# Six places instead of four for the split parameters of a state-space kernel

## The chip, the core and the metric

The kernel runs on one core of a Trainium2 chip. The metric is the device time of one execution in microseconds (us). The kernel before took 372.38 us (median of three runs, 372.26 to 373.49). The engines are named as in the profile: PE (matrix products; PEld is its weight load), ACT (ScalarE), DVE (VectorE), POOL (GpSimd) and SP (SyncE, which only issues transfers here). Each engine works through its own instructions in their order; semaphores hold an instruction back until another engine or a transfer (DMA) has done its part.

## The reference, cut to what matters

Two branches are mixed with a gate per position: 2,048 positions, 640 channels, bfloat16.

```python
g = sigmoid((x * gate_w).sum(-1, keepdims=True))
# a: attention over 8 positions, 2 apart; 32 heads of 20 channels
qkv = x @ wqkv;  a = softmax(q . k[pos - 2*w]) weighted v  @ wo
# b: state-space convolution, N = 192 states a channel
logdA = exp(log_dt) * (A_re + 1j * A_im)
K = Re(einsum(C, exp(logdA * l), exp(log_dt) * B))      # l = 0 .. 2047
b = irfft(rfft(x padded) * rfft(K padded)) + x * Dskip
return g * a + (1 - g) * b
```

(The middle lines are shortened to their meaning.) The parameters A, B and C are 640 x 192 each, and the change concerns what is made of them before K can be computed.

## The kernel before

**Parameters.** `SSMParams.build` (L573 on) brings the complex parameters into a form of phase and size for every channel and state: `tau`, `x1` (phase), `xa`, `xl` (size) and `at` (angle), each a float32 tile of 128 x 960 (five blocks of 128 channels by 192 states). PE will need them in bfloat16, so each is split into two or three bfloat16 pieces whose sum is the value. `piece` (L650 to 659) makes one of the twelve pieces in three steps:

- ACT rounds the current value to a bfloat16 tile `pc` (L655, a copy of 128 x 960),
- SP stores this tile in the DRAM tensor `Sprm` (L657, 240 KB),
- where another piece follows, DVE subtracts `pc` from the value (L659); what is left goes into a scratch tile `s` and is the next piece's value.

The `pc` tiles come from the pool `sp_pc` (L582). A place is free again when its transfer to `Sprm` has landed and the subtraction has read it; the next copy that is given this place waits for both. Which place that is, is settled when the program is built, by the order in which places are given back in the program; it isn't a strict rotation. With the order of this kernel, the twelve copies wait for transfers as follows (counted in ACT's order):

| copy | 1 to 4 | 5 | 6 | 7 | 8 | 9 | 10 | 11 | 12 |
|---|---|---|---|---|---|---|---|---|---|
| waits for the transfer of piece | none | 1 | 4 | 2 | 5 | 6 | 7 | 3 | 8 |

**What stands beside it.** In the same stretch PE turns the input `x` with products with the identity (`ar` <- `ident`,`xn`, L252; evicted by ACT or DVE into `bufA`), computes the gate's sums (L268), and projects q, k and v: groups of five matmuls of 128 x 512 into a PSUM tile `tb` (L339, in `plan_late`, L317 on). There are two `tb` places; each group is evicted by ACT (L512) or DVE (L514) into `pv` or `prj`, and POOL's queue stores what belongs together (L354) into `qS`, `kS` and `vS` in DRAM and loads windows from there (`qc` and `kc` L381, `vc` L389). DVE's first products q times k are `prod` (L395). When all twelve pieces have landed, SP loads the matrices `L` from `Sprm` (L765), PE multiplies them with constants (L792), and ACT turns these into sines and exponentials (L804, L806) from which K is summed. The Fourier transforms and the mix with the gate follow in `fft_conv` (L1009 on).

**What sets the order.** A planner (`Plan`, L68 on) holds every step as a task with an engine, an expected duration, a due time, dependencies and the places that it takes and gives back, and plays them through (`order`, L98). Its list `SLOTS` (L75) has its own number of places for each pool, `"pc": 4` among them. `emit` (L198) then writes the instructions in the played order and ties every engine to it, so no engine leaves the order at run time.

Of the kernel before, what the change touches and what calls it, by code (L numbers as in the profile page):

```python
# [572 lines left out]
class SSMParams:  # L573
# [5 lines left out]
    def build(self, ctx, tc, pl, A_re, A_im, B_re, B_im, C_re, C_im, log_dt, gate_w, ident, gw_sb, pa, xl, wl):  # L579
        nc = tc.nc  # L580
        pin = ctx.enter_context(tc.tile_pool(name="sp_in", bufs=1, side="right"))
        pcs = ctx.enter_context(tc.tile_pool(name="sp_pc", bufs=4, side="right"))  # L582
        SH = [128, 5, NST]
        t = {}

# [765 lines left out]
```

## Time and profile before

One execution was profiled. Its views give times from the span's start.

| | |
|---|---|
| profiled execution | 372.98 us, span of its instructions 371.2 us |
| median of the runs | 372.38 us |
| busy share of the span: PE, DVE, ACT, POOL | 82%, 86%, 82%, 27% |
| mean granted clock of PE | 0.93 of full speed |
| transfers `Sprm` <- `pc` | 12, issued from 24.2 to 64.1 us, 3.5 to 8.4 us from issue to landing, median 7.3 |
| the copies `pc`, L655 | 12, about 1.00 us each, from 23.2 to 63.1 us |
| DMA share in the stages 30 to 40, 40 to 50, 50 to 60 us | 0.89, 1.06, 0.83 |

A timeline lists an engine's instructions by start; in brackets stands how long the engine was idle before one and what ended the wait. A table of waits sums these. The windows view gives the busy time of each engine within chosen stretches, the granted clock there (1.00 is full speed) and how busy the 16 DMA engines were; its share can pass 1 in this count. Busy time of PE is modelled at its ends, so that a gap in its timeline tells more than its share.

### The profile page before, as it was taken

To read this page: it belongs to the slowest core of one execution; us is meant where nothing else is said; L and a number is where in the kernel's file an instruction comes from. 1 tells how busy PE (TensorE), PEld (TensorE's weight loads), DVE (VectorE), ACT (ScalarE), POOL (GpSimd) and SP (SyncE) were. 2 spreads that over 40 slices of the span, in tenths; PEclk is the share of its full clock that TensorE was granted. 3 is DMA by queue.
4 is the path that set the end of the run, shared out by engine and by line. 5 is a ranking of instruction groups with operands and counts; after the bars stand their busy time and mean duration, and the time that the engine had idled before them with its cause. 6 is when DMAs were issued, how large, how long until landed. Compare 5 with 4: busy or idle time off the path is not lost. (4 is left out here: it accounts for less than half of the span.)

```text
span 371.2 us, 12265 instructions
## 1 busy us (share of the span) xinstructions
PE 303.6 (82%) x5286; PEld 176.0 (47%) x5286; DVE 319.6 (86%) x431; ACT 305.4 (82%) x417; POOL 98.4 (27%) x134
## 2 busy tenths in 40 slices
PE   0189499999999998896888888988989899988770
PEld 0155265444454444443344444546656656557660
DVE  2897969866999999999798999999889759999972
ACT  1499877468899899999799989979878698998881
POOL 8932332302003012236157001010110014310032
PEclk9999789999999998997595699989999999999985
DMA  8957988765346362759567833443464039943037
GB/s 259 369 153 190 255 214 245 226 193 171 106 96 183 116 131 85 166 124 216 90 199 158 195 92 86 104 92 106 124 225 145 13 113 221 252 93 72 4 91 197
DMA packets 53130, 57.26 MB, mean 154 GB/s; under 512 B 32596, under 2 KB 44692, under 8 KB 52820
## 3 DMA queue, kind: packets, MB, share of 16 engines
q0 software_dynamic: 8784, 31.20, 31.4%
q1 hardware_dynamic: 42260, 24.43, 26.0%
q10 hardware_dynamic: 2032, 0.85, 0.9%
q8 instruction: 41, 0.67, 0.8%
q14 instruction: 13, 0.11, 0.1%
HBM read 36.69 MB, written 19.77 MB: 152 GB/s over the span
## 5 line engine op out<-in xcount | busy, mean ns | idle before, releaser
L339 PE MATMUL tb<-bufA 128*128 128x512 bf16 x300 | 75.0, 391 | 6.2 <-ACT pv L512 4.8
L792 PE MATMUL ar<-Rarg,L 64*128 64x304 bf16 (+1 forms) x480 | 58.1, 299 | 15.4 <-ACT big L806 7.1
L804 ACT ACTIVATE big<-ar 128x608 bf16<-128x608 int16 x96 | 59.8, 679 | 10.1 <-PE ar L792 9.1
L395 DVE TENSOR_TENSOR prod<-qc,kc 128x2048 bf16<-128x2048 bf16 x40 | 47.3, 1218 | 5.7 <-PE lg L401 3.3
L339 PEld LDWEIGHTS <-bufA 128*128 128x128 bf16 x300 | 33.1, 121 | 37.1 <-issue 15.4
L806 ACT ACTIVATE big<-ar 128x864 bf16<-128x864 f32 x60 | 49.1, 900 | 1.4 <-PE ar L792 1.1
L462 DVE TENSOR_TENSOR pv<-vc,asb 128x2048 bf16<-128x2048 bf16 x40 | 47.3, 1217 | 1.5 <-PE tb L468 1.3
L792 PEld LDWEIGHTS <-L 64*128 64x128 bf16 x480 | 22.2, 97 | 50.4 <-issue 46.5
L1053 PEld LDWEIGHTS <-PHI 128*128 128x128 bf16 x288 | 26.2, 97 | 17.1 <-issue 8.7
L486 PE MATMUL tb<-wo_sb,oT 128*128 128x320 bf16 x160 | 28.7, 314 | 0.2
L845 PE MATMUL kps<-qq,pt 128*32 128x22 bf16 (+1 forms) x2560 | 26.4, 176 | 2.5 <-issue 1.1
L389 POOL DMA_DIRECT2D vc<-vS x16 | 11.7, 749 | 62.6 <-DVE pv L462 57.3
L845 PEld LDWEIGHTS <-pt 128*32 128x32 bf16 (+1 forms) x2560 | 22.7, 93 | 10.7 <-issue 7.3
L512 ACT ACTIVATE prj<-tb 128x512 bf16<-128x512 f32 x30 | 17.7, 597 | 7.8 <-PE tb L339 7.8
L468 PE MATMUL tb<-pv,ind 128*64 128x512 bf16 (+1 forms) x192 | 22.7, 358 | 1.6 <-DVE pv L462 1.3
L829 DVE TENSOR_TENSOR qq<-big 128x1408 bf16<-128x1408 bf16 x24 | 21.2, 882 | 0.0
L512 ACT ACTIVATE sp_k<-fp 128x1280 bf16<-128x1280 f32 x14 | 17.3, 1237 | 3.9 <-PE fp L1053 3.4
L252 PE MATMUL ar<-ident,xn 128*128 128x128 bf16 x80 | 8.3, 273 | 14.4 <-DMA xn<-in_A_x_dram 13.9
L1053 PE MATMUL fp<-bufA,PHI 128*128 128x320 bf16 x112 | 17.5, 298 | 3.2 <-ACT sp_k L512 2.2
L486 PEld LDWEIGHTS <-oT 128*128 128x128 bf16 x160 | 13.9, 101 | 8.4 <-issue 2.2
L401 PE MATMUL lg<-prod,ind 128*32 128x512 bf16 x160 | 16.6, 426 | 1.4 <-DVE prod L395 1.4
L827 DVE TENSOR_TENSOR pt<-big 128x1024 bf16<-128x1024 bf16 x24 | 16.4, 685 | 1.3 <-PE kps L845 0.7
(174 smaller groups left out, 599.7 us busy)
## 6 DMA issues: line engine op xcount, KB each, us to landing
vc<-vS POOLq DMA_DIRECT2D x16, 327.5 KB, 5.8
PHI<-c_phi POOLq DMA_DIRECT2D x8, 384.0 KB, 5.7
Sprm<-pc SPq DMA_DIRECT2D x12, 240.0 KB, 7.3
L<-Sprm SPq DMA_DIRECT2D x80, 36.0 KB, 3.6
kc<-kS POOLq DMA_DIRECT2D x8, 337.5 KB, 4.9
xn<-in_A_x_dram SPq DMA_DIRECT2D x4, 640.0 KB, 9.1
qc<-qS POOLq DMA_DIRECT2D x8, 320.0 KB, 5.6
Usb<-in_A_x_dram POOLq DMA_DIRECT2D x8, 320.0 KB, 5.2
```

Of the source, the lines that this page charges most:

```text
L339: nc.tensor.matmul(ppf, self.wq[:, kt, which * D + e:(which + 1) * D:5], self.xT[:, c0 // 1024, kt, c0 % 1024:c0 % 1024 + SC], start=(kt = ...
L395: nc.vector.tensor_tensor(b[e][:], b["qc"][:, e, :].unsqueeze(1).to_broadcast([128, W, C]), win(b["kc"][:, e, :], 0, W, DIL, C), ALU.mult)
L462: nc.vector.tensor_tensor(b["pv", e][:, :, :, k, :], for_e, aw, ALU.mult)
L468: nc.tensor.matmul(b["op", e][64 * a:64 * a + 64, 0:n, :], self.twin, b["pv", e][:, a, w, 0:n, :], start=(w == 0), stop=(w == HV - 1), ski ...
L486: nc.tensor.matmul(apf[:, :320], b["oT"][:, e, i * 128:(i + 1) * 128], wo_sb[:, e, hf * 320:(hf + 1) * 320], start=(e == 0), stop=(e == 4))
L512: nc.scalar.activation(o, i, ACT.Identity)
L792: nc.tensor.matmul(ar[:, g2, a0:a0 + ncol], L[rows, sb, gp, l0:l0 + 128], R[rows, c0:c0 + ncol], start=True, stop=True, tile_position=(64 ...
L804: nc.scalar.activation(dst[:, 2 * gp:2 * gp + 2, sub, :], ar[:].bitcast(I16)[:, :, 0:2 * SW:2], ACT.Sin, scale=SCL)
L806: nc.scalar.activation(dst[:, 2 * gp:2 * gp + 2].rearrange("p g s n -> p g (s n)"), ar[:, :, 0:2 * EW], ACT.Exp)
L829: nc.vector.tensor_tensor(qq[:], trg[:, :, KI:].rearrange("p a (v m) -> p a v m", v=2), exq[:, :, KI:].unsqueeze(2).to_broadcast([128, 32, ...
L845: nc.tensor.matmul(kps[32 * g:32 * g + 32, h, NM * ql:NM * ql + NM], pt[rows, k, v, :], qq[rows, k, v, :], start=(g not in started), stop= ...
L1053: nc.tensor.matmul(o.rearrange("p (c x) -> p c x", x=32), phis[fb][:, fl, kind, :], B[:, :, 2 * f1 + ri].rearrange("p c q g -> p c (q g)") ...
```

## The change

The pool of the `pc` tiles gets six places instead of four:

```diff
-        pcs = ctx.enter_context(tc.tile_pool(name="sp_pc", bufs=4, side="right"))
+        pcs = ctx.enter_context(tc.tile_pool(name="sp_pc", bufs=6, side="right"))
```

The planner's own `"pc": 4` stays, so the order that it plays stays too: in the built programs all five engines have the same instructions in the same order. Each place is 1,920 bytes in each partition, so the pool takes 3,840 bytes more. The addresses of ten of the twelve `pc` tiles differ; nothing else moved. In the built program the copies now wait for transfers so:

| copy | 1 to 6 | 7 | 8 | 9 | 10 | 11 | 12 |
|---|---|---|---|---|---|---|---|
| waits for the transfer of piece | none | 1 | 4 | 2 | 5 | 6 | 7 |

## The prediction, made before the changed kernel ran

> **What bounds the kernel now.** I read the page's slices first: from 37 to 55 us PE has a dip (4 tenths) and the granted clock two low slices (7 and 8 tenths), while DVE and ACT stay busy. So I asked for the waits of the stretch 18 to 80 us, and from there the timelines of ACT, PE and DVE. The waits (engine and line, what it waited for, us in total, times, longest):
>
> ```profile
> PE tb L339 <- ACT pv L512: 4.8, 3, 4.4
> ...
> ACT pc L655 <- DMA Sprm<-pc: 1.0, 1, 1.0
> ```
>
> PE's longest stop, 4.4 us, waits for an eviction by ACT. Of the twelve piece copies (L655) exactly one waits for a transfer, for 1.0 us. ACT's timeline (start, length, operation, in brackets the idle time before it and its releaser) shows that the one stands ahead of the other:
>
> ```profile
> 36.28 1.00 ACT L655 ACTIVATE pc<-s 128x960 bf16<-128x960 f32 x1
> 37.19 0.58 ACT L512 ACTIVATE pv<-tb 128x512 bf16<-128x512 f32 x1
> 37.79 1.28 ACT L635 ACT_TABLE_LOAD   x1
> 39.08 1.00 ACT L635 ACTIVATE at<-t 128x960 f32<-128x960 f32 x1
> 41.05 1.00 ACT L655 ACTIVATE pc<-s 128x960 bf16<-128x960 f32 x1 [0.96 <-DMA Sprm<-pc]
> 41.96 0.99 ACT L655 ACTIVATE pc<-x 128x960 bf16<-128x960 f32 x1
> 42.85 1.06 ACT L512 ACTIVATE pv<-tb 128x512 bf16<-128x512 f32 x2
> ```
>
> The sixth copy starts at 41.05 after 0.96 us of waiting; the seventh and two evictions of `tb` stand behind it on ACT. PE's timeline:
>
> ```profile
> 37.82 1.24 PE L339 MATMUL tb<-bufA 128*128 128x512 bf16 x5 [0.24 <-ACT pv L512]
> 43.48 4.43 PE L339 MATMUL tb<-bufA 128*128 128x512 bf16 x10 [4.42 <-ACT pv L512]
> 47.70 1.06 PE L252 MATMUL ar<-ident,xn 128*128 128x128 bf16 x8
> 48.55 1.66 PE L339 MATMUL tb<-bufA 128*128 128x512 bf16 x5
> 50.05 0.61 PE L252 MATMUL ar<-ident,xn 128*128 128x128 bf16 x8
> 50.50 2.32 PE L339 MATMUL tb<-bufA 128*128 128x512 bf16 x10
> ```
>
> Both `tb` places are full from 39.06 on; PE goes on at 43.48, right after the first of the two evictions, and from there it shows no gap until 82.15. In the stages 54 to 78 us it is busy 24.00 of 24 us at clock 1.00. So PE bounds this stretch, and its start at 43.48 hangs on ACT, which hangs on the transfer. Ten matmuls took 4.43 us here; 25 took 5.63 at 54.66, about half the time each. The windows show why (start:end, length, busy PE, PEld, DVE, ACT, POOL, then granted clock, DMA share, GB/s):
>
> ```profile
> 39.15:42.56 3.41, 0.00 (x0) 0.00 (x0) 3.27 (x5) 2.45 (x3) 2.48 (x4) 1.00 1.09 237
> 42.56:45.97 3.41, 2.49 (x6) 0.85 (x6) 3.31 (x4) 3.35 (x6) 0.00 (x0) 0.50 1.03 284
> 45.97:49.39 3.42, 3.42 (x15) 1.74 (x14) 3.39 (x4) 1.63 (x3) 0.91 (x1) 0.50 1.05 216
> 49.39:52.80 3.41, 3.41 (x28) 2.08 (x27) 0.49 (x2) 2.83 (x4) 1.59 (x2) 1.00 0.63 184
> 141.55:144.96 3.41, 1.82 (x76) 1.08 (x74) 3.34 (x6) 3.38 (x5) 0.00 (x0) 1.00 0.55 181
> ```
>
> The clock is 0.50 from 42.56 to 49.39. Such stretches begin and end on a grid of 3.41 us (the next begins at 144.96, 28 steps after 49.39). It fell after a step without PE work, also after one with 1.82 us of it; it stayed low after steps with 2.49 and, at 175.68, 3.07 us, and rose after 3.42, and twice after 3.38. The stop thus costs PE twice: 4.42 us, and then 5.91 us at half speed (43.48 to 49.39).
>
> **The change, part by part.**
> *Order:* the built program of the changed kernel has the same instructions in the same order on all five engines (the planner's own count of places stays four). Only the places of `pc` move in memory, and what copies wait for.
> *The sixth copy.* In the kernel before it waits for the fourth piece's transfer (issued at 33.86):
>
> ```profile
> DMA to landing us min/median/max: 7.1/7.1/7.1
> ```
>
> 33.86 + 7.1 = 40.96, and the copy starts at 41.05. With six places the fifth and sixth copies take fresh ones, and only DVE is waited for, whose last input (L659, 38.11 + 1.15) was there at 39.26. ACT is then free at 40.08, and a following ACTIVATE of this shape starts 0.09 before the end of the one ahead (41.05 + 1.00 against 41.96). Gain: 0.96 + 0.09, taken as 1.05 us.
> *The other copies.* The fifth's transfer had long landed: nothing. The seventh to twelfth now wait for pieces 1, 4, 2, 5, 6, 7 instead of 2, 5, 6, 7, 3, 8. The longest landing of all twelve transfers is 8.4 us, so the latest of them, piece 7 (issued 42.97), is there by 51.4, and its place is wanted at 63.11; piece 4 (40.96) is wanted at 51.65, piece 6 (50.5) at 60.88. No new wait; the nearest margin is 10 us.
> *Transfers.* Pieces six and seven are issued (SP, L657) 1.05 us earlier, at 41.0 and 41.9, into steps whose DMA share is above 1. They may hold up the stores and loads of POOL's queue; that is weighed below.
> *What is late next.* ACT: seventh copy, evictions, all without a wait, 1.05 earlier. PE starts at 42.43. Up to 50.5 it needs only evictions that ACT then does earlier too. The next engine to limit it is DVE:
>
> ```profile
> 48.60 1.16 DVE L632 SCALAR_TENSOR_TENSOR at<-t,at 128x960 f32<-128x960 f32 x1
> 52.69 1.16 DVE L659 TENSOR_TENSOR s<-s,pc 128x960 f32<-128x960 f32 x1 [2.92 <-ACT pc L655]
> ```
>
> DVE stands idle 2.92 us for a copy by ACT that stands behind PE's work, so a lead of up to 2.9 us meets no work of DVE. After that every engine works on what these three made, in a fixed order, with no rest that belongs to none of them: the lead should reach the end.
> *The clock.* If the grid lies as in this profile, PE starts at 42.43, fills the step 42.56 to 45.97 (3.41 of 3.41, where 2.49 was too little), and the next runs at full clock. At half clock PE then does until 45.97 what it did until 47.02; the 2.37 us left to 49.39 shrink by 1.18. Lead: 1.05 + 1.18 = 2.2 us. Where the grid lies in another execution this profile can't say. Moving it by up to one step and counting half-clock time for a stop from 39.06 to 43.48 and one to 42.43 (falls after a step with under about 1.8 us of work, rises after more than 2.6 to 3.3; my estimates from the rows above): the clock part lies between a loss of 0.5 (half-clock time 1 us longer) and a gain of 1.7 (no fall at all), about 0.4 in the middle. So the lead is 0.55 to 2.75, about 1.45.
>
> *A rule beside these rows.* The Trainium skill, "TensorE: Matmul & The Clock Gate", Part 1: The HAM clock gate, says that the clock is halved after at least one idle window of about 3.4 us, and that the windows run free of the kernel's start. The second half agrees with the grid and would let its position differ from run to run; the first does not cover the fall at 144.96, after 1.82 us of work. The same section warns against fitting a kernel to a count of cold matmuls, which speaks against the 1.18. By its rule of whole idle windows the changed stop, 3.37 us, would cost no fall.
>
> **Sum.** From this profile: 372.98 (span 371.2 and 1.8 around it) - 2.2 = 370.8. From the median, 0.6 below that execution, with the middle lead: 372.38 - 1.45 = 370.9. I take 370.9.
>
> **Rivals.**
> *A: the lead is taken back by transfers (about 372.4).* DVE's first `prod` starts at 63.59; its `qc` load was issued at 55.37 and landed 6.4 later, at 61.76: 1.8 us of margin. DMA share is 0.95 in 54 to 60. For it: the store ahead of it (`qS`, 3.7 us) and the load may take longer when the work before them is pressed together. Against: both are issued behind evictions that come earlier, and the bytes are the same. If landings stay at their old times, `prod` can still come 1.8 earlier; the lead is gone only if they land as much later as it is long.
> *B: the clock does not fall at all.* The stop of 3.37 us leaves no whole step of the grid idle. All 5.91 us at half clock would go, 2.95 us; with 1.05 that is 4.0, which DVE's 2.92 cuts off: 372.98 - 2.9 = 370.1. Against it: the fall after 1.82 us of work. (This is what the quoted rule gives.)
> *C: slower.* The writes of pieces six and seven come 1.05 earlier against POOL's store of `kS` (issued 39.37, 7.6 us) and through it the `kc` loads, `qS` and `qc`. It decides from where `qc` lands after 63.59, 1.8 us later than now; with 3 us later `prod` starts 1.2 later: 374.2. For it: DMA shares of 1.03 to 1.09. Against: two writes of 240 KB at 237 GB/s are 2.1 us in all, POOL has idle time before each issue (2.6 us before `qc`), and PE's own matmuls don't wait for `qc` before 65.98.
> *D: the added places go unused.* Excluded by the built program: copy six has no wait for a transfer.
>
> **How the numbers follow.** A difference under 0.3% (1.1 us) can't be told from none. Forecast 70%: 57 of these with a lead over 1.1, 13 with one of 0.55 to 1.1. A 17%, B 7%, C 6%. Faster: 57 + 7 = 64%; same: 13 + 17 = 30%; slower: 6%. Range: leads of 2.6 to 0.1 from the median, 369.8 to 372.3; it leaves out C, the far end of B and part of A.
>
> **What would show it.** Right: no line "ACT pc L655 <- DMA Sprm<-pc" in the waits; the sixth copy right behind `at`, about 1 us earlier; PE's stop about 3.4 instead of 4.42; PE at the `tb` group of 50.50 by 1 to 2.2 us earlier; `prod` and the first `ar` of L792 (78.87) earlier by as much; the granted clock low for one step or none after the stop. Wrong: a wait of the copy for something else, a PE stop as long as before, or a lead at 50 us that `prod`, L792 or the last stage no longer has.

## The result, and the profile after

| | before | after |
|---|---|---|
| median of the runs on the same chip | 372.54 us (20 runs, 369.52 to 375.61) | 370.53 us (20 runs, 367.79 to 373.74) |
| profiled execution (span) | 372.98 us (371.2) | 369.61 us (367.8) |
| mean granted clock | 0.93 | 0.937 |

The ratio is 0.9952 with an interval of 0.9929 to 0.9976: 0.9 to 2.6 us faster, 1.8 in the middle. (The ratio is taken without slow executions and the medians with them, so the medians are 2.0 us apart.) The forecast of 370.9 us lies 0.4 us from the median. Single executions in this table lie up to some 3 us to either side of their median, so the 3.4 us between the two profiled executions are one draw, not the effect.

The waits of after in the stretch 18 to 80 us (engine and line, what it waited for, us in total, times, longest):

```profile
POOL qc L381 <- DMA qS<-pv: 4.5, 1, 4.5
...
PE tb L339 <- ACT pv L512: 4.0, 3, 3.3
```

There is no line any more in which a copy waits for `Sprm`. PE's longest stop fell from 4.4 to 3.3 us. The first line has no counterpart in before, and comes back below. The timeline of ACT in after:

```profile
36.80 0.58 ACT L512 ACTIVATE pv<-tb 128x512 bf16<-128x512 f32 x1
...
38.69 1.00 ACT L635 ACTIVATE at<-t 128x960 f32<-128x960 f32 x1
39.60 0.99 ACT L655 ACTIVATE pc<-s 128x960 bf16<-128x960 f32 x1
40.49 0.99 ACT L655 ACTIVATE pc<-x 128x960 bf16<-128x960 f32 x1
41.38 1.06 ACT L512 ACTIVATE pv<-tb 128x512 bf16<-128x512 f32 x2
```

The sixth copy (39.60) starts 0.91 us after `at` starts, where it was 1.97: 1.06 us are gone, and the seventh copy and the evictions follow without a gap. (`at` itself starts 0.39 us earlier in this execution. That difference is there from 30 us on, ahead of the sixth copy; in the other kernels' profiles the same difference to before lies between -0.5 and 0.6 us. It is taken off wherever a lead is called net.) PE in after:

```profile
37.42 1.24 PE L339 MATMUL tb<-bufA 128*128 128x512 bf16 x5 [0.24 <-ACT pv L512]
42.01 3.71 PE L339 MATMUL tb<-bufA 128*128 128x512 bf16 x10 [3.35 <-ACT pv L512]
...
47.53 2.32 PE L339 MATMUL tb<-bufA 128*128 128x512 bf16 x9
```

The ten matmuls behind the stop took 3.71 us instead of 4.43, and the group that started at 50.50 starts at 47.53, 2.97 us earlier, net 2.58. The windows of the clock's grid in after (start:end, length, busy PE, PEld, DVE, ACT, POOL, granted clock, DMA share, GB/s):

```profile
38.04:41.45 3.41, 0.62 (x3) 0.24 (x2) 3.27 (x4) 3.40 (x5) 3.25 (x5) 1.00 1.16 259
41.45:44.86 3.41, 2.85 (x7) 1.03 (x7) 3.33 (x4) 3.35 (x6) 0.00 (x0) 0.50 1.00 260
44.86:48.28 3.42, 3.37 (x28) 2.25 (x28) 3.36 (x4) 2.58 (x5) 1.01 (x2) 1.00 1.07 250
```

The clock is low for one step instead of two. PE works 2.85 us at half speed, where it was 5.91. DVE in after:

```profile
49.72 1.16 DVE L659 TENSOR_TENSOR s<-s,pc 128x960 f32<-128x960 f32 x1 [0.35 <-ACT pc L655]
...
60.78 2.35 DVE L395 TENSOR_TENSOR prod<-qc,kc 128x2048 bf16<-128x2048 bf16 x2
```

Of the 2.92 us that DVE stood idle ahead of this subtraction, 0.35 are left. `prod` starts at 60.78 instead of 63.59 and the first `ar` of L792 at 76.06 instead of 78.87: both 2.81 earlier, net 2.4. From 60 to 140 us the lead (taken from the starts of the same DVE instruction) stays at 2.8. Behind that the two executions have their half-clock stretches at different places, and the lead wanders: 2.5 at 170 us, 4.5 from 200 to 250, 3.1 from 310 on, with short peaks above.

### The profile page after: what moved, and what is told of

Same layout as the page of the kernel before. It is cut to its first block, busy times and chain, and to the rows that moved or that the text cites. A ratio compares the mean times of both kernels' runs of the same rounds, so it can differ in the third digit from the quotient of the medians.

```text
span 367.8 us, 12246 instructions
## 1 busy us (share of the span) xinstructions
PE 299.3 (81%) x5269; PEld 174.1 (47%) x5286; DVE 320.0 (87%) x431; ACT 305.1 (83%) x417; POOL 97.2 (26%) x134
## 5 line engine op out<-in xcount | busy, mean ns | idle before, releaser
L339 PE MATMUL tb<-bufA 128*128 128x512 bf16 x283 | 71.4, 387 | 7.0 <-ACT pv L512 4.0
L792 PE MATMUL ar<-Rarg,L 64*128 64x304 bf16 (+1 forms) x480 | 58.4, 300 | 15.2 <-ACT big L806 6.4
L804 ACT ACTIVATE big<-ar 128x608 bf16<-128x608 int16 x96 | 59.8, 679 | 8.2 <-PE ar L792 7.0
L792 PEld LDWEIGHTS <-L 64*128 64x128 bf16 x480 | 22.5, 97 | 49.9 <-issue 45.5
L252 PE MATMUL ar<-ident,xn 128*128 128x128 bf16 x80 | 7.5, 255 | 13.9 <-DMA xn<-in_A_x_dram 13.4
L1053 PE MATMUL fp<-big,PHI 128*128 128x320 bf16 x112 | 17.5, 298 | 0.0
```

The source lines that it names most:

```text
L339: nc.tensor.matmul(ppf, self.wq[:, kt, which * D + e:(which + 1) * D:5], self.xT[:, c0 // 1024, kt, c0 % 1024:c0 % 1024 + SC], start=(kt = ...
L792: nc.tensor.matmul(ar[:, g2, a0:a0 + ncol], L[rows, sb, gp, l0:l0 + 128], R[rows, c0:c0 + ncol], start=True, stop=True, tile_position=(64 ...
L804: nc.scalar.activation(dst[:, 2 * gp:2 * gp + 2, sub, :], ar[:].bitcast(I16)[:, :, 0:2 * SW:2], ACT.Sin, scale=SCL)
L1053: nc.tensor.matmul(o.rearrange("p (c x) -> p c x", x=32), phis[fb][:, fl, kind, :], B[:, :, 2 * f1 + ri].rearrange("p c q g -> p c (q g)") ...
```

## The experiments

The theory: the sixth copy's wait for one transfer is the whole of it. It holds up nothing on ACT that is urgent in itself, but two evictions that stand behind it, for which PE waits. The rivals: that something else which six places bring makes the gain (other waits of later copies, other addresses, other transfer times), and that the gain is mostly the clock's, so that any work that keeps the clock up is worth as much. Each ratio below is against the kernel before on the same chip. In kernels with lines added, the line numbers are 1 to 5 higher than those of before.

### Five places, and six of which two copies share one

```diff
 five places
-        pcs = ctx.enter_context(tc.tile_pool(name="sp_pc", bufs=4, side="right"))
+        pcs = ctx.enter_context(tc.tile_pool(name="sp_pc", bufs=5, side="right"))
 the wait put back: in addition to that
+        pc1 = ctx.enter_context(tc.tile_pool(name="sp_pc1", bufs=1, side="right"))
...
-                t[k] = pcs.tile(SH, BF16, name="pc")
+                t[k] = (pc1 if i in (1, 11) else pcs).tile(SH, BF16, name="pc")
```

In the second kernel `i in (1, 11)` are the fourth and the sixth copy in ACT's order: there are six places as in after, but the sixth copy waits for the fourth piece's transfer again.

> Five places in the pool, nothing else. In this program the first five copies take fresh places, and the sixth waits for the transfer of the first piece, which landed some 14 us before. Theory (the gain is the wait of the sixth copy, and the clock that follows from PE's shorter stop): the sixth copy starts right behind the arctangent, PE's stop is about 3.4 us, and the time is that of six places, ratio 0.992 to 0.998 to the kernel before. Rival (it takes both added places, because a later copy's wait or the place in memory counts): a ratio nearer to 1, above 0.998.

> Six places as in the change, but two of the twelve pieces, the fourth and the sixth copy, share one of them, so that the sixth copy again waits for the fourth piece's transfer. Theory: all of the gain is gone, ratio 0.998 to 1.002 to the kernel before, an ACT wait of about 1 us before the sixth copy, a PE stop of about 4.4 us. Rival (the other copies' places or the memory layout bring part of it): ratio 0.995 to 0.998.

Five places: 371.07 us (12 runs) against 372.07, ratio 0.9955 (0.9919 to 0.9991). The wait put back: 372.91 us (12 runs), ratio 1.0011 (0.9975 to 1.0048). Both lie where the theory had them, though the ends of the two intervals overlap (0.9975 to 0.9991). In the kernel with the wait put back, ACT and PE show the old picture:

```profile
41.67 1.00 ACT L656 ACTIVATE pc<-s 128x960 bf16<-128x960 f32 x1 [1.13 <-DMA Sprm<-pc]
```

```profile
44.10 3.85 PE L339 MATMUL tb<-bufA 128*128 128x512 bf16 x10 [4.58 <-ACT pv L512]
```

Six places with this wait show no gain, and five without it are worth as much as six (0.9955 against 0.9952). Times that scatter so much don't exclude a small share of the sixth place, the later copies or the addresses; but the stop of PE comes and goes with this wait alone (4.58 us with it, 3.35 without), and so, as far as the medians tell, does the gain.

Five places also show the clock. The windows on that execution's grid:

```profile
37.18:40.59 3.41, 1.78 (x15) 1.03 (x13) 3.31 (x4) 3.38 (x5) 3.23 (x5) 1.00 1.12 249
40.59:44.00 3.41, 1.45 (x7) 0.82 (x7) 3.34 (x4) 3.41 (x6) 0.49 (x1) 1.00 0.98 221
44.00:47.41 3.41, 3.32 (x28) 2.20 (x27) 3.34 (x4) 3.41 (x6) 0.44 (x1) 1.00 1.04 275
```

PE's stop is 3.35 us long, as in after, but the grid cuts it in two, and the clock does not fall at all. With the same stop, then, after lost one step and this execution none: where the grid lies differs from execution to execution.

### Three places

```diff
-        pcs = ctx.enter_context(tc.tile_pool(name="sp_pc", bufs=4, side="right"))
+        pcs = ctx.enter_context(tc.tile_pool(name="sp_pc", bufs=3, side="right"))
```

> Three places. The fifth copy now waits for the fourth piece's transfer (landing near 41 us, wanted at 36.3), and the seventh for the fifth's. Theory: ACT's two added waits, about 4.6 us at the fifth copy and some 5 to 8 us at the seventh less what they overlap, go through PE to the end: 5 to 10 us slower than before, ratio 1.014 to 1.027. Rival (waits of these copies are mostly covered by work of other engines): under 1.005.

375.39 us (4 runs) against 371.69, ratio 1.011 (1.0058 to 1.0162): slower, but less than expected. ACT shows why:

```profile
40.69 1.00 ACT L655 ACTIVATE pc<-s 128x960 bf16<-128x960 f32 x1 [4.54 <-DMA Sprm<-pc]
41.60 0.58 ACT L512 ACTIVATE pv<-tb 128x512 bf16<-128x512 f32 x1
...
44.40 0.99 ACT L655 ACTIVATE pc<-s 128x960 bf16<-128x960 f32 x1
```

The fifth copy waits 4.54 us for a transfer, but the sixth no longer does: by then the place that it is given is free. One long wait takes the place of the later ones instead of adding to them. ACT's `at` runs 4.4 us behind that of before; the sixth copy and PE's ten matmuls behind its stop are 3.3 us late, and from 60 us on the work is 2.4 us late.

### Work put into PE's stop

If the clock makes the gain, unread matmuls in the stop should bring it with four places too. Behind the five matmuls after which PE stops, two kernels get 15 unread bfloat16 products of 128 x 512 into the free PSUM place `lg` (with weight loads, 30 instructions on PE). A third kernel has as many added instructions, but ahead of 15 us, far from the stop.

```diff
 filled, four places or six (in plan_late, behind the group)
+                        if sc == 0 and which == 0 and e == 0:
+                            fl = ps.tile([128, W, 64], F32, name="lg")
+                            for _k in range(15):
+                                nc.tensor.matmul(fl[:].rearrange("p a b -> p (a b)"), self.wq[:, 0, 0:640:5], self.xT[:, 0, 0, 0:SC], start=True, stop=True)
 early, six places (in SSMParams.build)
+        for _k in range(15):
+            nc.tensor.matmul(lt[:, 1, 0:128], ident, ident, start=True, stop=True)
```

> Four places, but behind the last tb group before PE's stop 15 more matmuls of 128x512 write a PSUM bank that nobody reads (added work, its result unused), some 3.2 us at full clock, so that PE keeps working for most of the stop and starts the next group no later. Theory: the clock does not fall after the stop, and the 2 to 3 us that half clock cost are won, up to the 2.92 us at which DVE limits: ratio 0.992 to 0.996, clock 1.00 from 42 to 50 us; the ACT wait of 1 us stays. Rival (half clock costs nothing that lasts, DVE or transfers take it back): ratio 0.998 to 1.002.

> Six places and the same 15 unread matmuls as in the run with four places. Theory: the wait of 1.05 us is won beside the clock, until DVE's own chain limits: 0.3 to 1.05 us below the filled kernel with four places, ratio 0.990 to 0.994 to the kernel before, and below six places alone by 0.5 to 1.5 us. Rival (six places gained through the clock alone): the same time as the filled kernel with four places.

> Six places, and 15 unread matmuls (30 instructions with their weight loads) on PE before 15 us, where PE has nothing to do. In the filled kernels PE stood still some 3 us near 172 us without waiting for any semaphore, while a 16 KB transfer of instructions was under way. Theory (the 30 added instructions move the places at which PE's program is reloaded, one of them into a stretch of busy transfers): the same stop comes here, though the work before 60 us is that of six places alone: 372.5 to 374.5 us, about 3 us above six places alone. Rival (the stop came from the work done earlier, or from the filled gap itself): no such stop, 370 to 371.5 us.

Four places filled: 374.64 us (12 runs) against 372.07, ratio 1.0075 (1.0043 to 1.0106), slower. Six places filled: 373.99 us (12 runs), ratio 1.0046 (1.0015 to 1.0077). Both expectations fell, though the stretch that the first spoke of went as expected: the clock stayed at 1.00, and with four places the work of 60 to 140 us is 2.9 us ahead of before. The lead falls first at 172 us, in a stop that the kernel before does not have. PE with four places filled:

```profile
171.14 1.00 PE L796 MATMUL ar<-Rarg,L 64*128 64x216 bf16 x7
175.47 0.59 PE L796 MATMUL ar<-Rarg,L 64*128 64x216 bf16 x3 [3.32 <-issue]
```

"issue" means that no semaphore held PE. What PE waits for then can be read from another queue. Each of the 14 profiles has 41 packets of a kind that the DMA view calls "q8 instruction", of 16 KB each, 0.67 MB in all: some 64 bytes for each of PE's 10,555 matmuls and weight loads in after. They are taken to be PE's program, which is loaded piece by piece while it runs. Two things in the kept traces bear this out. First, between 15 and 352 us PE stands still for "issue" 25 times for 0.4 us or more, all profiles together, and each time it goes on 1.3 to 1.6 us after such a packet ends. Here the packet runs from 172.55 to 174.06, and PE goes on at 175.47. Second, PE stops earlier in its program by just as many matmuls as were added ahead of the stop. Near 250 us every kernel that stops for 0.4 us or more does so at a place that depends on this number alone:

| matmuls added (each with a weight load) | kernels | PE stops behind | earlier by |
|---|---|---|---|
| 0 | after, five places, the wait put back, four places with evictions first | the 7th matmul of `bp` (a group of 16) | - |
| 6 | three float32 products, four places and six | the 1st of this group | 6 matmuls |
| 8 | four float32 products, four places and six | the 4th of the five `tb` ahead of the group | 8 |
| 15 | four places filled, six filled, early | the 61st of the 64 `kps` ahead of these five | 15 |

```profile
251.22 0.47 PE L1271 MATMUL bp<-F1c,kc 64*128 64x128 bf16 x9 [0.72 <-issue]
...
253.78 0.19 PE L847 MATMUL kps<-qq,pt 128*32 128x22 bf16 x3 [2.46 <-issue]
```

(The first line is after, the second the early kernel. The float32 products are those of the next section.) So the added instructions do not move a packet into a crowded moment: after has one at 172 us too, from 171.91 to 173.30, and doesn't stop. They bring PE sooner to the place where it needs that packet, 15 matmuls and 15 weight loads sooner, while the packet ends no earlier (173.3 to 174.1 us in the three kernels).

The early kernel confirms that the stop needs no filled gap: nothing is put into PE's stop, and up to 60 us it runs as the changed kernel does, yet it takes 374.22 us (12 runs) against 371.69, ratio 1.0066 (1.0041 to 1.0092), and stands still 2.26 us for "issue" at the same matmul, 172.7 to 174.9. The 30 instructions cost some 3.5 to 4 us (374.0 and 374.2 against the 370.5 of six places), wherever they stand. The stops near 172 us (2.3 to 3.3 us) and near 250 us (0.8 to 2.5, against 0.7 in after) are the part of it that is shown; how the rest comes about, by way of the clock or otherwise, is not. Nor is the stop alone the whole loss: the profiled execution with four places filled has it and took 371.12 us, the fastest of its twelve.

### The same with few instructions

Float32 products take longer (0.9 us for each of 128 x 512 here), so three or four of them fill the stop. The trace shows each as two weight loads and two matmuls (`x8` below), so they add 12 or 16 instructions to PE's program, and not 3 or 4 as the expectations have it.

```diff
 in plan_late, behind the group; range(4) or range(3), four places or six
+                        if sc == 0 and which == 0 and e == 0:
+                            fl = ps.tile([128, W, 64], F32, name="lg")
+                            for _k in range(4):
+                                nc.tensor.matmul(fl[:].rearrange("p a b -> p (a b)"), self.wq[:, 0, 0:256].bitcast(F32), self.xT[:, 0, 0, 0:2 * SC].bitcast(F32), start=True, stop=True)
```

> Four places; the stop of PE filled with 4 unread float32 matmuls of 512 columns (about 0.85 us each by estimate, one instruction each) instead of 15 in bfloat16, so the program grows by 4 instructions instead of 30. Theory: the clock does not fall after the stop, no new stop near 172 us, and the loss to half clock is won, ratio 0.991 to 0.996 to the kernel before. Rival (the clock after the stop doesn't count at the end): 0.998 to 1.002.

> Four places, PE's stop filled with 3 unread float32 matmuls instead of 4 (3 added instructions). The filled kernel with four places came out at the time of the kernel before, though it led by 3 us between 60 and 140 us in its profile. Theory A (the half-clock stretch after the stop is worth about 2 us at the end, and that result was chance or due to the 4 added instructions): ratio 0.992 to 0.996. Theory B (what the clock gives back here is lost again in the later stretches of half clock, which lie on the same grid): 0.998 to 1.002 again.

> Six places; PE's stop filled with 3 such float32 matmuls. Theory: the wait and the clock together, as far as DVE's own chain lets them (2.9 us against the kernel before as profiled): ratio 0.989 to 0.994, 0.3 to 1.2 us below the filled kernel with four places. Rival (with the clock up, DVE limits and the wait is worth nothing): the same as the filled kernel with four places.

> Six places, PE's stop filled with 4 unread float32 matmuls instead of 3. Theory A: 0.989 to 0.993. Theory B: the gain of the six places alone, 0.994 to 0.997.

| places | float32 products | median, us | before, us | ratio (interval) |
|---|---|---|---|---|
| 4 | 4 | 371.65 (12 runs) | 371.69 | 1.0003 (0.9972 to 1.0034) |
| 4 | 3 | 370.86 (12 runs) | 371.97 | 0.9962 (0.9928 to 0.9996) |
| 6 | 3 | 370.84 (12 runs) | 371.69 | 0.9959 (0.9928 to 0.9990) |
| 6 | 4 | 371.82 (12 runs) | 371.97 | 0.9987 (0.9951 to 1.0023) |

The stop at 172 us is gone, but for 0.72 us with six places and four products. PE of the kernel with four places and four products:

```profile
37.70 1.24 PE L339 MATMUL tb<-bufA 128*128 128x512 bf16 x5 [0.24 <-ACT pv L516]
38.77 3.60 PE L344 MATMUL lg<-bufA 128*128 128x512 f32 x8
42.88 2.32 PE L339 MATMUL tb<-bufA 128*128 128x512 bf16 x10 [0.51 <-ACT pv L516]
```

The ten matmuls behind the stop take 2.32 us: full clock. In their profiled executions all four kernels lead the one of before by 2.7 to 3.8 us between 65 and 140 us, as much as after or more, and none of them has more of it at the end than after has; the first and the last can't be told from before. So a clock that is held up by force does bring the lead at 140 us without the change (four places, three products), but the theory that this lead then reaches the end does not hold for them as it should: 0.991 to 0.996 was expected of the first and 0.989 to 0.994 of the third, and the middle of the last misses both of its forecasts.

The profiles show where the lead goes, if not all of the reason. Between 250 and 270 us it falls by 3.3 to 3.6 us in these four, and by 1.6 and 1.7 in after and with five places. These four stop there for their program for 1.5 to 2.0 us (the table above), the other two for 0.7 and 0.8; behind it the clock is at half for two steps of the grid in these four and for one in the other two. Two such steps, and a fall of 3.3 us, also come with the wait put back, which has no added instruction, so the added instructions explain a part at most.

### The evictions first

Nothing is added here. In the list that `emit` writes out, the two evictions on ACT (tasks `lev0` and `lev1`) move ahead of the sixth copy (`mk11`). No other engine's order changes.

```diff
-        for t in self.order():
+        L = self.order()
+        at = {t.name: t for t in L}
+        for x, y in ((("lev0", "mk11"), ("lev1", "mk11")) if "lev0" in at else ()):
+            L.remove(at[x])
+            L.insert(L.index(at[y]), at[x])
+        for t in L:
```

> Six places, and on ACT the two tb evictions that PE waits for are moved ahead of the sixth and seventh copies; nothing is added and no other engine's order changes. PE's stop should fall from about 3.4 to 1.6 us, the clock should mostly stay up, the two copies come 1.06 us later, which DVE and SP don't need sooner. Theory A (PE's start after the stop and the clock both reach the end, up to DVE's margin of 2.9 us): ratio 0.989 to 0.993. Theory B (the clock's part is lost again later): 0.993 to 0.997, little or nothing beyond six places alone.

> Four places, with the two tb evictions moved ahead of the sixth and seventh copies as in the kernel before this one. The sixth copy waits for the fourth piece's transfer again. Theory (the wait cost what it did because PE's evictions stood behind it on ACT): PE starts after the stop as early as with six places and evictions first, the copy's own wait falls to about 0.5 us, and the time is within 0.4% of that kernel: ratio 0.988 to 0.995 to the kernel before. Rival (the wait counts on its own, through the copies or the pieces behind it): 0.995 to 1.000.

With six places: 368.74 us (6 runs) against 371.97, ratio 0.9898 (0.9851 to 0.9946). With four: 369.35 us (12 runs) against 371.88, ratio 0.9936 (0.9903 to 0.9968). ACT and PE with six places:

```profile
39.54 1.07 ACT L517 ACTIVATE pv<-tb 128x512 bf16<-128x512 f32 x2
40.50 1.00 ACT L660 ACTIVATE pc<-s 128x960 bf16<-128x960 f32 x1
```

```profile
40.17 2.32 PE L344 MATMUL tb<-bufA 128*128 128x512 bf16 x10 [1.56 <-ACT pv L517]
```

PE stops for 1.56 us instead of 3.35, the clock stays up from 40 to 50 us, and the work of 65 to 140 us is 3.7 us ahead of before (net 3.3). With four places ACT looks the same, and the sixth copy has no wait in brackets:

```profile
39.92 1.06 ACT L517 ACTIVATE pv<-tb 128x512 bf16<-128x512 f32 x2
40.87 1.00 ACT L660 ACTIVATE pc<-s 128x960 bf16<-128x960 f32 x1
```

The two evictions fill the time that the copy had to wait for its place (a wait of 0.5 us was expected to be left; the profile shows none). That is the theory's last test: four places are enough if nothing urgent stands behind the copy. Evictions first with six places has the lowest ratio of all that ran, and the intervals of it and of the change alone (0.9851 to 0.9946, 0.9929 to 0.9976) overlap by only 0.0017. Between six places and four it makes no difference that these runs can tell.

## Why the prediction was right, point by point

- **The sixth copy, 1.05 us.** Measured 1.06 in the two timelines. Five places and the wait put back show no share of anything else in the change, as far as their scatter allows.
- **PE's stop, 3.37 us.** Measured 3.35, in after and with five places.
- **"No new wait".** Held; no copy waits for a transfer.
- **The clock, -0.5 to +1.7, 0.4 in the middle; 1.18 if the grid lies as in before.** The grid lay otherwise: PE started again 0.56 us into a low step instead of 0.13 us ahead of one, and the low time shrank by 3.06 us of PE work (5.91 to 2.85), worth 1.53 at half speed. With 1.06 this gives the net 2.6 measured at 50 us; that it is near the 2.2 worked out for the old grid is luck. In another draw (five places) the clock did not fall at all. So a range and no single value was right. On average the clock is up longer: the mean granted clock over all 20 executions of after is 0.939, and 0.931 to 0.933 in four sets of 17 to 35 executions of before, some 4 to 6 us less at half clock. What this is worth at the end can't be told so closely: the 1.8 us (0.9 to 2.6) of the ratio less 1.06 leave -0.2 to 1.5. The 0.4 in the middle is within that, but that the forecast came within 0.4 us of the median is in part luck too.
- **DVE caps the lead at 2.9 us.** Of DVE's idle 2.92 us after used 2.57. In the kernels that keep the clock up (five places, six with 15 matmuls or with three or four products, both with the evictions first), the net lead from 65 to 140 us is 3.2 to 3.3 us, whatever PE's own start was. So there is a cap, some 0.3 higher than the one row said.
- **The lead reaches the end.** Held for after, for five places and for the evictions first in their ratios, within what scatters. It is the weakest step: the filled kernels had the same lead at 140 us and kept less of it, and in the profile of the evictions first with six places, too, it falls from 3.7 at 140 us to 1.8 from 270 us on. The lead of a single profile behind 140 us is therefore no measure of the gain.
- **Rival A and C, transfers.** Their mechanism showed, below its threshold. In after POOL's wait for `qS` is 4.5 us, a line that the stretch did not have before: the store of `qS` took 5.6 us to land instead of 3.7 (4.2, and a wait of 3.1, with the wait put back), so that the load of `qc` landed at 59.8, only 1.0 us ahead of `prod` (1.8 in before). `prod` did not wait, so it cost nothing.
- **Rival B, no fall of the clock.** The rule behind it did not hold: in after the clock did drop behind a step with 0.62 us of PE work, although no whole step of the grid was idle. The Trainium skill, "TensorE: Matmul & The Clock Gate", Part 1: The HAM clock gate, asks for at least one idle window; the measurement decides, and says that a step with little work is enough. The 1.45 us of work with five places were enough to keep the clock, while 1.82 us at 141.55 in before were not, so busy time alone is not the measure either. As an outcome B does occur, with another position of the grid (five places), and the cap of the point above then cuts it off much as forecast.

## What to carry to other kernels

A wait costs what stands behind it in its engine's queue. Here a wait of 1 us for a buffer that nobody needed soon held up two evictions for which PE stood still; it can be taken away by one more place, or by moving the urgent work ahead of it, which here also shortened the part of the stop that is no wait for a buffer (1.56 us instead of 3.35) and gave the lowest times, at the edge of what these runs can tell apart. Adding work in order to fill a stop is not free, even where the engine is idle: the added instructions lengthen a program that must itself be loaded. Look at the whole span, not at the stretch that was filled.

## What the runs showed of the hardware that was not expected

- PE can stand still for its own program. The 25 stops for "issue" of 0.4 us or more in the 14 profiles all end 1.3 to 1.6 us after a 16 KB packet of the queue taken to be PE's program, and they come earlier in the program by the number of matmuls added ahead of them.
- 30 added instructions on PE, in the stop or ahead of 15 us, cost 3.5 to 4 us of 370. All three kernels with them stop for 2.3 to 3.3 us near 172 us; among the others no PE wait of this kind there is longer than 0.7 us.
- The clock's grid of 3.41 us has no fixed position against the program: low stretches or steps begin at 42.56 in before, 41.45 in after, and at 40.59 with five places. The same stop of 3.35 us cost one low step in after and none with five places. Over the 35 executions of before that were run beside five places, the slower ones tend to have the lower granted clock (correlation -0.6), so the clock is likely a part of why executions of one kernel scatter.
- Three places cost 4 us and not the sum of the waits that were expected: behind the one wait of 4.54 us the next two copies found their places free.
